# A token-parallel layout for the upper 64 features, and a deeper lag of the second matmul, in a dynamic convolution followed by a squared-ReLU feed-forward

## The chip, the core and the metric

The kernel runs on one core of a Trainium2 chip. A core has five engines that work side by side, each through its own list of instructions in order: TensorE (PE; its weight loads are shown apart as PEld), VectorE (DVE), ScalarE (ACT), GpSimd (POOL) and SyncE (SP, which only issues DMAs here). They meet through semaphores. The metric is the device time of one execution in microseconds. Before the change it is 881.08 us (median of three runs, 879.11 to 881.46).

## The reference

For 8 sequences of 4096 tokens with 192 features, each token has 8 heads of 7 weights. The weights pass through a softmax, and each output feature is the weighted sum of the feature over the token and the six before it. The result goes through a feed-forward layer with a squared ReLU.

```python
w = np.exp(weight_gen - max);  w = w / (sum(w) + 1e-09)       # [B, S, 8, 7]
out[b, s, h, g] = sum_k w[b, s, h, k] * x_pad[b, s + k, h, g]  # 8 heads of 24 features
h = np.maximum(out @ w_in, 0.0)                                # 192 -> 2048
return h * h @ w_out                                           # 2048 -> 192
```

## The kernel before

The 32768 tokens are cut into 64 blocks of 512, eight to a sequence. For each block the kernel does these stages, named as in the code.

- **Softmax** (lines 106 to 175). It runs for a whole sequence ahead of its blocks, in chunks of 8 of the 38 rows that a partition holds. `exp` is on ScalarE, `total` (a reduction) and `recip` on VectorE, and `scale` on GpSimd: it multiplies by the reciprocal and scatters the result into `v_big` (`v_small` for the first sequence, which comes in four parts of 8 rows with 14 rows each, halo included). `store` writes that to DRAM (`vd`). A chunk is done in each of a sequence's blocks 0 to 4, after the ReLUs of the block's last group.
- **st_load** fetches the block's features `xt` (on GpSimd's queue) and its weights `wr` (on SP's queue), three blocks ahead.
- **st_band** (VectorE) multiplies weights by a mask into five banded matrices `bd`, one for each stretch of about 100 tokens.
- **st_conv** (TensorE) does the convolution as 32-column matmuls against `bd`. Features 0 to 127 fill the first PSUM bank of `yp`. Features 128 to 191 are computed twice, once into partitions 0 to 63 and once into 64 to 127 of the second bank: that is 80 matmuls for a block. `st_y_evac` (ScalarE) copies both banks to SBUF as `y`.
- **st_mm1** multiplies by `w_in` in 16 chunks of 128 outputs, two chunks to a buffer `h` of two PSUM banks (a chunk pair, `fp` 0 to 7). Each chunk takes one 512-column matmul over the lower 128 features (`w_a`, line 274) and one over the upper 64 (`w_b`, line 282). The upper matmuls use half of the array's rows, and the two chunks of a pair take different halves and run at the same time.
- **st_relu** (ScalarE, line 293) and **st_sq** (VectorE, line 299) make `t1` and then `g` of a chunk pair.
- **st_mm2** (TensorE, line 310) multiplies by `w_out`: 8 matmuls of 192 columns for a chunk pair, summed in one buffer `o` of two banks. **st_o_evac** (VectorE) copies it out, and SP stores it.

The chunk pairs go in groups of (0,1,2), (3,4,5) and (6,7). There is no scheduler: the order is that of the loop in lines 368 to 404, engine by engine. TensorE does MM1 of a group, and then MM2 of the group before it. Three `h` buffers are shared in turn by the chunk pairs and `yp`, so MM1 of a pair needs the ReLU of the pair three places earlier to be done. A `g` has eight buffers, `bd` two, `o` one.

## Time and profile before

| what | value |
|---|---|
| median of 3 runs | 881.08 us (879.11 to 881.46) |
| the profiled execution | 880.54 us, of which 878.8 us is the span from first to last instruction |
| TensorE matmul busy | 796.8 us (91%), 11264 matmuls, each with a weight load of its own |
| VectorE busy | 638.2 us (73%) |
| ScalarE busy | 568.2 us (65%) |
| GpSimd busy | 147.6 us (17%) |
| mean granted TensorE clock | 0.991 |

The page gives busy shares over the whole span. A timeline (instructions in order of time, with what each engine waited for) shows the single block. A row of a timeline reads: start, duration, engine, line, operation, output and input tiles, shape, count, and in brackets the idle time just before it with what ended it. A duration of several merged matmuls includes the last one's way through the array, so the pace is taken from starts.

### The profile page before, as it was taken

To read this page: it belongs to the slowest core of one execution; us is meant where nothing else is said; L and a number is where in the kernel's file an instruction comes from. 1 tells how busy PE (TensorE), PEld (TensorE's weight loads), DVE (VectorE), ACT (ScalarE), POOL (GpSimd) and SP (SyncE) were. 2 spreads that over 40 slices of the span, in tenths; PEclk is the share of its full clock that TensorE was granted. 3 is DMA by queue.
4 is the path that set the end of the run, shared out by engine and by line. 5 is a ranking of instruction groups with operands and counts; after the bars stand their busy time and mean duration, and the time that the engine had idled before them with its cause. 6 is when DMAs were issued, how large, how long until landed. Compare 5 with 4: busy or idle time off the path is not lost.

```text
span 878.8 us, 25261 instructions
## 1 busy us (share of the span) xinstructions
PE 796.8 (91%) x11264; PEld 520.6 (59%) x11264; DVE 638.2 (73%) x979; ACT 568.2 (65%) x616; POOL 147.6 (17%) x140
## 2 busy tenths in 40 slices
PE   0678999989998999998999899998999899999997
PEld 0345666655665666665665665665666566666665
DVE  2567787687768787678777778668776878767674
ACT  0346666666676666666666666666667666666764
POOL 5332120123002220112201212012300212000000
PEclk9889999999999999999999999999999999999999
DMA  9522372232713254033622237223271225433111
GB/s 165 116 47 39 60 156 54 37 68 57 141 46 50 52 116 103 25 67 53 144 56 57 35 63 156 48 44 67 51 148 46 45 57 92 78 47 68 41 38 37
DMA packets 123789, 63.03 MB, mean 72 GB/s; under 512 B 87713, under 2 KB 121120, under 8 KB 122912
## 3 DMA queue, kind: packets, MB, share of 16 engines
q0 software_dynamic: 44480, 17.57, 18.0%
q1 hardware_dynamic: 79200, 43.84, 17.4%
q8 instruction: 88, 1.44, 0.7%
q14 instruction: 21, 0.17, 0.1%
HBM read 49.60 MB, written 29.36 MB: 90 GB/s over the span
## 4 chain that ended last, share of the span: by engine, by line
PE 45%; DVE 24%; ACT 14%; issue 13%; DMA 2%; POOL 1%; ACTq 0%; SPq 0%; DVEq 0%; POOLq 0%
PE o L310 23%; PE h L274 12%; DVE g L299 9%; ACT t L293 8%; DVE bd L223 7%; PE h L282 7%; ACT y L264 4%; DVE o_sb L320 4%; PE yp L251 3%; DVE ssum L146 3%; DVE rcp L152 2%; ACT wg L139 2%; DMA wr<-vd 1%; POOL mask L92 0%; DMA vd<-v_small 0%
## 5 line engine op out<-in xcount | busy, mean ns | idle before, releaser
L293 ACT ACTIVATE t<-h 128x1024 f16<-128x1024 f32 x512 | 489.8, 1023 | 282.3 <-PE h L282 264.9
L299 DVE TENSOR_TENSOR g<-t 128x1024 f16<-128x1024 f16 x512 | 383.1, 775 | 102.1 <-ACT t L293 102.1
L310 PE MATMUL o<-w_o,g 128*128 128x192 f16 x4096 | 380.5, 248 | 47.8 <-DVE g L299 41.6
L310 PEld LDWEIGHTS <-g 128*128 128x128 f16 x4096 | 331.8, 98 | 116.4 <-DVE g L299 81.0
L274 PE MATMUL h<-y,w_a 128*128 128x512 f16 x1024 | 259.7, 382 | 8.1 <-ACT t L293 6.9
L223 DVE TENSOR_TENSOR bd<-wr,mask 128x832 f16<-128x832 f16 (+2 forms) x320 | 171.0, 582 | 17.9 <-DMA wr<-vd 17.9
L160 POOL TENSOR_TENSOR v_big<-wg,rcp 128x448 f16<-128x448 f32 (+1 forms) x35 | 81.6, 2330 | 474.2 <-DVE rcp L152 474.2
L274 PEld LDWEIGHTS <-w_a 128*128 128x128 f16 x1024 | 97.9, 98 | 91.0 <-issue 20.0
L282 PE MATMUL h<-y,w_b 64*128 64x512 f16 x1024 | 144.5, 381 | 0.0
L146 DVE TENSOR_REDUCE ssum<-wg 128x64 f32<-128x448 f32 (+2 forms) x39 | 24.7, 633 | 110.0 <-ACT wg L139 110.0
L282 PEld LDWEIGHTS <-w_b 64*128 64x128 f16 x1024 | 34.3, 94 | 97.2 <-issue 82.2
L251 PE MATMUL yp<-bd,xt 128*32 128x104 f16 (+7 forms) x5120 | 71.1, 210 | 21.6 <-DVE bd L223 21.6
L251 PEld LDWEIGHTS <-xt 128*32 128x32 f16 (+3 forms) x5120 | 59.5, 93 | 48.8 <-issue 35.5
L213 POOL DMA_DIRECT2D xt<-in_x_dram x56 | 49.7, 887 | 170.8 <-PE yp L251 170.8
L264 ACT CAST y<-yp 128x1024 f16<-128x1024 f32 x64 | 65.1, 1018 | 19.3 <-PE yp L251 19.3
L320 DVE COPY o_sb<-o 128x768 f32<-128x768 f32 x64 | 60.8, 950 | 3.9 <-PE o L310 1.0
L139 ACT ACTIVATE wg<-wg 128x448 f32<-128x448 f32 (+2 forms) x39 | 23.6, 610 | 2.0 <-DMA wg<-in_weight_gen_dram 2.0
L152 DVE RECIPROCAL rcp<-ssum 128x64 f32<-128x64 f32 (+2 forms) x39 | 22.1, 566 | 1.7
L160 POOL TENSOR_TENSOR v_small<-wg,rcp 128x336 f16<-128x336 f32 (+1 forms) x7 | 13.0, 2025 | 15.9 <-issue 13.9
L211 POOL DMA_DIRECT2D xt<-in_x_dram x8 | 6.0, 751 | 0.0
L205 POOL DMA_DIRECT2D xt<-in_x_dram x8 | 4.8, 606 | 0.0
L92 POOL TENSOR_SCALAR_AFFINE_SELECT mask<-mask 128x104 f16<-128x104 f16 (+2 forms) x6 | 3.1, 509 | 0.4
(14 smaller groups left out, 12.4 us busy)
## 6 DMA issues: line engine op xcount, KB each, us to landing
out_dram<-o_sb SPq DMA_DIRECT2D x64, 384.0 KB, 2.8
xt<-in_x_dram POOLq DMA_DIRECT2D x56, 240.0 KB, 4.0
wg<-in_weight_gen_dram SPq DMA_DIRECT2D x6, 1064.0 KB, 8.2
wr<-vd SPq DMA_DIRECT2D x56, 80.0 KB, 3.0
vd<-v_big SPq DMA_DIRECT2D x7, 512.0 KB, 3.3
wg<-in_weight_gen_dram SPq DMA_DIRECT2D x4, 392.0 KB, 3.7
xt<-in_x_dram POOLq DMA_DIRECT2D x8, 192.0 KB, 6.2
wg<-in_weight_gen_dram SPq DMA_DIRECT2D x1, 896.0 KB, 5.8
```

What stands on the lines that cost most here:

```text
L146: nc.vector.tensor_reduce(out=self.ssum[:, i], in_=self.wg[:, i], axis=AxisX, op=AluOp.add)
L160: eng.tensor_tensor(out=bass.AP(tensor=v.tensor, offset=v.offset + i0 * H * SL, ap=[list(v.ap[0]), [H * SL + 1, n], [SL, H], [H * SL, KK]] ...
L213: eng.dma_start(out=dst, in_=rows(src, t0 + BASE, width))
L223: nc.vector.tensor_tensor(out=bd_t[j][:, H * lo : H * hi].rearrange("p (h m c) -> p h m c", h=H, c=SL), in0=wr_t[j][:, i].unsqueeze(2).bro ...
L251: nc.tensor.matmul(out=yp[p0 : p0 + m, ci, lo:hi], lhsT=x_t[j][:, i, 32 * q : 32 * q + m], rhs=bd[:, hb if later else ha, :], start=True, ...
L264: nc.scalar.copy(out=y, in_=yp_t[j])
L274: nc.tensor.matmul(out=h[:, jj, :], lhsT=w_a[:, fc * P : (fc + 1) * P], rhs=y[:, 0, :], start=True, stop=False,)
L282: nc.tensor.matmul(out=h_t[(j, fp)][:, jj, :], lhsT=w_b[r0 : r0 + LO, fc * P : (fc + 1) * P], rhs=y[r0 : r0 + LO, 1, :], start=False, stop ...
L293: nc.scalar.activation(out=t1, in_=h_t[(j, fp)], func=ActF.Relu)
L299: nc.vector.tensor_tensor(out=g, in0=t1, in1=t1, op=AluOp.mult)
L310: nc.tensor.matmul(out=o[:, c // 2, (c % 2) * Dm : (c % 2 + 1) * Dm], lhsT=g_t[(j, fp)][:, jj, c * P : (c + 1) * P], rhs=w_o[:, fc, :], st ...
L320: nc.vector.tensor_copy(out=o_sb, in_=o_t[j][:, :, 0 : 2 * Dm])
```

## The change

Five things change together.

1. The two halves of the array's rows now hold the two halves of the block's tokens for the upper 64 features, not two copies of them. `st_conv` computes features 128 to 191 once: tokens 0 to 255 go to partitions 0 to 63, and tokens 256 to 511 to partitions 64 to 127. That is 64 matmuls for a block. `y` shrinks from 1024 to 768 columns. In MM1 each chunk now takes two 256-column matmuls over the lower features and two over the upper ones, and `h`, `t1` and `g` are laid out by token half.
2. MM2 of chunk pair 5 moves behind the next block's first MM1 group: the groups of MM2 are (0,1,2), (3,4) and, late, (5,6,7). `g` has six buffers instead of eight, `bd` three instead of two.
3. In the last group of MM1 the order on TensorE is lower features, convolution of the next block, upper features; ScalarE does `y`'s copy ahead of the two ReLUs.
4. For sequences after the first, the exponential comes after the first group's ReLUs, and reduction, reciprocal and scaling come on VectorE after the second group's squares. Chunks have 8, 8, 8, 4, 4, 4 and 2 rows from sequence 2 on (a sequence's own softmax now starts two blocks earlier), and 8, 8, 8, 8, 6 for sequence 1. GpSimd keeps only the scaling of the first sequence.
5. At the start, only the first part of the weights is loaded ahead of all; `w_in` and most masks come after the first block's loads, and the second block's loads ahead of parts 2 and 3.

```diff
+    TH = TB // 2
-    p_bd = ctx.enter_context(tc.tile_pool(name="p_bd", bufs=2))
+    p_bd = ctx.enter_context(tc.tile_pool(name="p_bd", bufs=3))
-    p_g = ctx.enter_context(tc.tile_pool(name="p_g", bufs=8))
+    p_g = ctx.enter_context(tc.tile_pool(name="p_g", bufs=6))
...
+    def conv_pieces():
+        for i in range(NT):
+            lo, hi = bounds[i], bounds[i + 1]
+            for later in (True, False):
+                for q in range(4):
+                    yield later, i, q, 32 * q, 0, lo, lo, hi
+                for half in (0, 1):
+                    a, b = max(lo, TH * half), min(hi, TH * (half + 1))
+                    if a < b:
+                        for q in (4, 5):
+                            yield later, i, q, 32 * (q - 4) + LO * half, 1, a - TH * half, a, b
...
-        y = p_y.tile([P, 2, TB], f16, name="y")
+        y = p_y.tile([P, TB + TH], f16, name="y")
-        nc.scalar.copy(out=y, in_=yp_t[j])
+        nc.scalar.copy(out=y, in_=yp_t[j].rearrange("p a c -> p (a c)")[:, 0 : TB + TH])
...
+    def st_mm1_lower(j, fps):
...
+                for half in range(2):
+                    nc.tensor.matmul(
+                        out=h[:, half, jj, :],
+                        lhsT=w_a[:, fc * P : (fc + 1) * P],
+                        rhs=y[:, half * TH : (half + 1) * TH],
+                        start=(jj == 0), stop=False, skip_group_check=True,
+                    )
+    def st_mm1_upper(j, fps):
...
+                for half, r0 in enumerate((0, LO)):
+                    nc.tensor.matmul(
+                        out=h_t[(j, fp)][:, half, jj, :],
+                        lhsT=w_b[r0 : r0 + LO, fc * P : (fc + 1) * P],
+                        rhs=y[r0 : r0 + LO, TB : TB + TH],
+                        start=False, stop=(jj == 1), skip_group_check=True,
+                        tile_position=(r0, 0),
+                    )
...
-        for s in parts[:2]:
-            s.load(nc.sync)
-        load_w_in()
+        parts[0].load(nc.sync)
...
+        softmax_whole(parts[0], (nc.vector, nc.gpsimd))
+        st_load(0)
+        load_w_in()
...
+        parts[1].load(nc.sync)
+        st_load(1)
...
+        softmax_whole(parts[1], (nc.gpsimd,))
+        for s in parts[2:]:
+            s.load(nc.sync)
+        st_load(2)
...
+            st_mm1_lower(j, G0)
+            st_mm1_upper(j, G0)
+            if j:
+                st_mm2(j - 1, LATE)
+            for fp in G0:
+                st_relu(j, fp)
+            if lo < hi:
+                nxt.exp(lo, hi)
...
+            st_mm1_lower(j, G1)
+            st_mm1_upper(j, G1)
+            st_mm2(j, (0, 1, 2))
+            for fp in G1:
+                st_relu(j, fp)
+                st_sq(j, fp)
+            if lo < hi:
+                nxt.recip(lo, hi)
+                nxt.scale(lo, hi, nc.vector)
...
+            st_mm1_lower(j, G2)
+            if more:
+                st_conv(j + 1)
+                st_y_evac(j + 1)
+            st_mm1_upper(j, G2)
+            st_mm2(j, (3, 4))
```

Three places in the order of instructions matter below. The first is VectorE at the end of a block in which a chunk of softmax is done (`ssum` and `rcp` are its sums and reciprocals, `wg` the weights; L299 and L328 are the squares). Before:

```order
L299 TENSOR_TENSOR g<-t_830 128x1024
L146 TENSOR_REDUCE ssum_478<-wg_257 128x64
L152 RECIPROCAL rcp_479<-ssum_478 128x64
L299 TENSOR_TENSOR g<-t_955 128x1024
L299 TENSOR_TENSOR g<-t_957 128x1024
L223 TENSOR_TENSOR bd<-wr,mask 128x832 x2
L223 TENSOR_TENSOR bd<-wr,mask 128x768
L299 TENSOR_TENSOR g<-t_1004 128x1024
L320 COPY o_sb<-o 128x768
L299 TENSOR_TENSOR g<-t_1006 128x1024
```

With the change:

```order
L328 TENSOR_TENSOR g<-t_1130 128x1024
L144 TENSOR_REDUCE ssum_288<-wg_241 128x64
L145 RECIPROCAL rcp_289<-ssum_288 128x64
L152 TENSOR_TENSOR v_big<-wg_241,rcp_289 128x8x8x7
L328 TENSOR_TENSOR g<-t_1238 128x1024
L328 TENSOR_TENSOR g<-t_1242 128x1024
L216 TENSOR_TENSOR bd<-wr,mask 128x832 x2
L216 TENSOR_TENSOR bd<-wr,mask 128x768
L328 TENSOR_TENSOR g<-t_1301 128x1024
L328 TENSOR_TENSOR g<-t_1303 128x1024
L332 COPY o_sb<-o 128x768
```

The scaling has joined the two other steps ahead of the squares of pairs 6 and 7, and the copy of `o` stands behind a second square.

The second is ScalarE around the last group of a block (CAST is `y`'s copy, L293 and L322 are the ReLUs, L139 and L140 the exponential). Before:

```order
L293 ACTIVATE t_593<-h 128x1024
L293 ACTIVATE t_718<-h 128x1024
L293 ACTIVATE t_720<-h 128x1024
L264 CAST y<-yp 128x1024
L139 ACTIVATE wg_257<-wg_257 128x448
L293 ACTIVATE t_767<-h 128x1024
```

With the change:

```order
L322 ACTIVATE t_624<-h 128x1024
L268 CAST y<-yp 128x768
L322 ACTIVATE t_732<-h 128x1024
L322 ACTIVATE t_736<-h 128x1024
L322 ACTIVATE t_795<-h 128x1024
L322 ACTIVATE t_797<-h 128x1024
L322 ACTIVATE t_799<-h 128x1024
L140 ACTIVATE wg_241<-wg_241 128x448
```

The ReLUs of pairs 6 and 7 (`t_732`, `t_736`) now stand behind the copy, and the exponential three ReLUs later.

The third is SP's queue at the start (`wg` are loads of softmax weights, the first four of them parts 0 to 3; `vd<-v_small` are the stores of finished parts; `wr` loads belong to blocks 0, 1 and 2 in turn). Before:

```order
L124 DMA wg_104<-in_weight_gen_dram 128x784
L124 DMA wg_106<-in_weight_gen_dram 128x784
L172 DMA vd<-v_small_99 128x512
L205 DMA wr<-vd 128x64
L211 DMA wr<-vd 128x4x64
L124 DMA wg_145<-in_weight_gen_dram 128x784
L124 DMA wg_147<-in_weight_gen_dram 128x784
L213 DMA wr<-vd 128x5x64
L172 DMA vd<-v_small_100 128x512
L213 DMA wr<-vd 128x5x64
L124 DMA wg_257<-in_weight_gen_dram 128x2128
```

With the change:

```order
L125 DMA wg_104<-in_weight_gen_dram 128x784
L165 DMA vd<-v_small_99 128x512
L198 DMA wr<-vd 128x64
L204 DMA wr<-vd 128x4x64
L125 DMA wg_139<-in_weight_gen_dram 128x784
L206 DMA wr<-vd 128x5x64
L165 DMA vd<-v_small_100 128x512
L125 DMA wg_231<-in_weight_gen_dram 128x784
L125 DMA wg_233<-in_weight_gen_dram 128x784
L206 DMA wr<-vd 128x5x64
L125 DMA wg_241<-in_weight_gen_dram 128x2128
```

Block 1's weights (the first `wr` row of five stretches) now stand ahead of parts 2 and 3, and those two loads stand behind the store of part 1.

224 lines of the change are left out of this document (99 added, 125 removed).

## The prediction

> **What bounds the kernel now.** First the page: TensorE is busy for 91% of the span, so the question is what it does in the rest.
>
> ```profile
> span 878.8 us, 25261 instructions
> PE 796.8 (91%) x11264; PEld 520.6 (59%) x11264; DVE 638.2 (73%) x979; ACT 568.2 (65%) x616; POOL 147.6 (17%) x140
> PE 45%; DVE 24%; ACT 14%; issue 13%; DMA 2%; POOL 1%; ACTq 0%; SPq 0%; DVEq 0%; POOLq 0%
> ```
>
> The last row is the chain that ended last: VectorE and ScalarE hold 38% of it, so TensorE waits for them regularly. The timeline gives the beat. Each block has one run of 80 convolution matmuls:
>
> ```profile
> 65.29 1.09 PE L251 MATMUL yp<-bd,xt 128*32 128x104 f16 x80
> ...
> 405.93 1.09 PE L251 MATMUL yp<-bd,xt 128*32 128x104 f16 x80
> 419.48 1.09 PE L251 MATMUL yp<-bd,xt 128*32 128x104 f16 x80
> 432.23 1.09 PE L251 MATMUL yp<-bd,xt 128*32 128x104 f16 x80
> 444.73 1.09 PE L251 MATMUL yp<-bd,xt 128*32 128x104 f16 x80
> ...
> 858.27 1.09 PE L251 MATMUL yp<-bd,xt 128*32 128x104 f16 x80
> ```
>
> The steps are 13.55, 12.74 and 12.50 us. From 65.29 (block 2) to 858.27 (block 63) are 61 steps and 792.98 us, 13.00 on average; 65.29 lies before and 20.53 behind. A 12.50 step looks like this:
>
> ```profile
> 435.24 1.46 PE L274 MATMUL h<-y,w_a 128*128 128x512 f16 x6
> 436.63 0.82 PE L282 MATMUL h<-y,w_b 64*128 64x512 f16 x6
> 437.06 2.86 ACT L293 ACTIVATE t<-h 128x1024 f16<-128x1024 f32 x3 [2.09 <-PE h L282]
> 437.38 1.49 PE L310 MATMUL o<-w_o,g 128*128 128x192 f16 x16
> 438.71 1.03 PE L274 MATMUL h<-y,w_a 128*128 128x512 f16 x4
> 439.96 0.59 PE L274 MATMUL h<-y,w_a 128*128 128x512 f16 x2 [0.23 <-ACT t L293]
> ```
>
> Each stage starts where the last one's stream ends, but for one wait. The third pair of the middle group needs the buffer that the third ReLU frees at 437.06 + 2.86 = 439.92. Four matmuls from 438.71 take 0.86, so TensorE is ready at 439.57 and loses 0.39. Without it a block is 12.11 us. The slow step has another wait:
>
> ```profile
> 406.95 2.15 PE L310 MATMUL o<-w_o,g 128*128 128x192 f16 x24
> 407.65 1.02 ACT L264 CAST y<-yp 128x1024 f16<-128x1024 f32 x1
> 408.55 0.60 ACT L139 ACTIVATE wg<-wg 128x448 f32<-128x448 f32 x1
> 409.18 0.62 DVE L146 TENSOR_REDUCE ssum<-wg 128x64 f32<-128x448 f32 x1 [2.76 <-ACT wg L139]
> 409.83 0.55 DVE L152 RECIPROCAL rcp<-ssum 128x64 f32<-128x64 f32 x1
> 410.30 2.72 DVE L299 TENSOR_TENSOR g<-t 128x1024 f16<-128x1024 f16 x2
> 410.57 2.43 POOL L160 TENSOR_TENSOR v_big<-wg,rcp 128x448 f16<-128x448 f32 x1 [10.64 <-DVE rcp L152]
> 413.07 0.83 PE L310 MATMUL o<-w_o,g 128*128 128x192 f16 x8 [1.16 <-DVE g L299]
> ```
>
> The squares of pairs 6 and 7 stand behind a reduction that waits for an exponential that waits for `y`'s copy. The two squares then take 2.72 us, with GpSimd's scaling beside them. MM2 waits 1.16 for the second. This is the 1.05 us between 13.55 and 12.50.
>
> **The change, part by part: matmuls.** The pace of a stream is its starts. Six matmuls of 512 columns span 1.46 us and four 1.03, so one takes (1.46 − 1.03)/2 = 0.215, and a single one's own length is 0.38. For 192 columns it is (1.49 − 0.25)/15 = 0.083, 0.25 being the single one's length in this row of the page (busy, mean ns of one; its weight loads below it):
>
> ```profile
> L310 PE MATMUL o<-w_o,g 128*128 128x192 f16 x4096 | 380.5, 248 | 47.8 <-DVE g L299 41.6
> L310 PEld LDWEIGHTS <-g 128*128 128x128 f16 x4096 | 331.8, 98 | 116.4 <-DVE g L299 81.0
> ```
>
> On the line through both, 256 columns take 0.109. The lower features cost 32 × 0.109 instead of 16 × 0.215, or +0.05 a block. The upper ones: three pairs of 512 start 0.22 apart ((0.82 − 0.38)/2); 256 columns less are 0.106 less, so 16 pairs at 0.114 stand against 8 at 0.22, +0.06. The convolution loses 16 of 80 matmuls, but these ran beside others in other column tiles; only in the stretch that spans both halves do two pieces of 48 columns run side by side where 96 ran, twice: −0.04. Modes of the array change as often as before (seven times a block). So 12.11 becomes **12.18**: the layout by itself saves TensorE nothing.
>
> That the 16 extra `w_b` loads are hidden rests on two rows:
>
> ```profile
> 427.87 0.11 PEld L282 LDWEIGHTS <-w_b 64*128 64x128 f16 x4 [0.42 <-issue]
> 428.11 0.10 PEld L282 LDWEIGHTS <-w_b 64*128 64x128 f16 x2
> ```
>
> Four loads are done in 0.11 us, and the next two start when the second pair of matmuls does and end 0.10 later, just inside the 0.114 that a pair will last. If the cover failed, see the rival below.
>
> **The buffer waits.** An `h` buffer is free 439.96 − 436.63 = 3.33 us after the upper matmuls of its group start. Into the middle group TensorE now arrives after 0.77 (six upper pairs and the change of mode; 437.38 − 436.63 = 0.75 before) + 24 × 0.083 + 8 × 0.109 = 3.63, with no wait: pair 5's MM2 fills the gap, and the 0.39 goes. Into the last group it arrives after 0.77 + 1.99 + 0.44 = 3.20 and waits **0.13**. Next late is the first group of the next block. ScalarE's copy starts some 1.10 after the convolution does. It costs between 1.02 (as before) and 0.82: 256 columns less at 0.00077 each, from the exponential's 0.60 for 448 columns and 0.858 for 784:
>
> ```profile
> L139 ACT ACTIVATE wg<-wg 128x784 f32<-128x784 f32 x4 | 3.3, 858 | 2.0 <-DMA wg<-in_weight_gen_dram 2.0
> ```
>
> I take 0.82, since duration follows size there. The ReLUs of pairs 6 and 7, ready earlier, stand behind it and follow at 0.92 ((2.86 − 1.02)/2); the second is over at 1.10 + 0.72 + 0.92 + 1.02 = 3.76 and its buffer free at 3.80. TensorE wants that buffer after the convolution (0.98: 406.95 − 405.93 = 1.02 with its change of mode, less 0.04), four upper pairs and a change (0.54), 16 matmuls of MM2 (1.32) and eight of 0.109 (0.88), at 3.72: a wait of **0.08**. A block comes to 12.18 + 0.21, say **12.40**; with a copy of 1.02 it would be 12.60.
>
> **The softmax.** GpSimd's scaling and its collision with the squares go. VectorE gets it instead. Its price is known from one instruction at the start, beside GpSimd's for the same shape:
>
> ```profile
> L160 POOL TENSOR_TENSOR v_big<-wg,rcp x35: 1864/2423/2466, 49.6 to 737.4; 128x448 f16<-128x448 f32 x28, 128x336 f16<-128x336 f32 x7
> L160 DVE TENSOR_TENSOR v_small<-wg,rcp x1: 2153/2153/2153, 6.8 to 6.8; 128x448 f16<-128x448 f32 x1
> ```
>
> The bounds are 0.62 (the reduction over as many elements) and 2.47 (GpSimd's longest); I take the row of the same engine and shape, 2.15. The Trainium skill, "VectorE: DVE Perf Modes", section "The TRN2 errata — SBUF-src ops pay a fixed extra latency per instruction", has fp32 tensor_tensor at (N + 151)/0.96 ns, an estimated 0.62 us here; the measured 2.15 for this scattered output speaks against it, and the page's figure would only take rival B away. VectorE's load in a plain block:
>
> ```profile
> 444.73:457.23 12.50, 12.27 (x179) 8.05 (x177) 8.70 (x14) 8.55 (x10) 0.85 (x1) 1.00 0.34 60
> ```
>
> (columns: PE, PEld, DVE, ACT, POOL busy.) 8.70 for its 14 instructions, plus 0.62 + 0.55 + 2.15 = 12.02 of 12.40 in a block with eight rows; there are 4 + 6 × 3 = 22 of these, and the others have room. Nobody waits: the 3.32 us start after the square of pair 5, delay the square of pair 7 to about 1.8 us into the next block, and MM2 of pair 7 comes at 3.5, since pair 5 and 6 go first; the bands and two squares behind it are done by 4.7, the copy of `o` by 5.6, and MM2 of pair 0, which needs them, starts at 6.3. The exponential (0.60) lies between the third ReLU, over 3.3 us after the first group's upper matmuls start, and the fourth, ready 0.43 (437.06 − 436.63) after the second group's do, at 0.77 + 1.99 + 8 or more matmuls of 0.109 and so past 4.5. So 61 steps of 12.40 are 756.4 instead of 793.0: **−36.6**.
>
> **The start.** Two rows of groups (a reduction of a whole part; a part's load, with its us to landing), then the timeline:
>
> ```profile
> L146 DVE TENSOR_REDUCE ssum<-wg 128x112 f32<-128x784 f32 x4 | 3.8, 951 | 5.1 <-ACT wg L139 5.1
> wg<-in_weight_gen_dram SPq DMA_DIRECT2D x4, 392.0 KB, 3.7
> ...
> 9.41 1.69 POOL L160 TENSOR_TENSOR v_small<-wg,rcp 128x336 f16<-128x336 f32 x1
> 24.23 1.01 ACT L264 CAST y<-yp 128x1024 f16<-128x1024 f32 x1 [19.32 <-PE yp L251]
> 28.03 3.71 POOL L160 TENSOR_TENSOR v_small<-wg,rcp 128x448 f16<-128x448 f32 x2 [13.93 <-issue]
> 37.10 1.56 DVE L223 TENSOR_TENSOR bd<-wr,mask 128x832 f16<-128x832 f16 x3 [5.96 <-DMA wr<-vd]
> 39.32 4.02 PE L310 MATMUL o<-w_o,g 128*128 128x192 f16 x24 [6.48 <-DVE g L299]
> 53.88 3.98 DVE L223 TENSOR_TENSOR bd<-wr,mask 128x832 f16<-128x832 f16 x3
> 59.38 4.00 PE L310 MATMUL o<-w_o,g 128*128 128x192 f16 x24 [4.32 <-DVE o_sb L320]
> ```
>
> GpSimd's scaling of six rows of part 0 no longer waits for the masks, but now collides with VectorE's of eight: in turn from 6.8 they end at 6.8 + 2.15 + 1.69 = 10.6 against 11.1, and I give the first load, now alone in its queue, another 0.5. So the first copy comes at 23.2. Block 1's bands no longer wait until 37.10 for `wr`. But part 2's load now stands behind the store of part 1, whose scaling ends near 30.7 (31.74 before). The load lands some 3.7 later, and its exponential (0.86) is in front of block 0's ReLUs on ScalarE: these start near 35.5. Reduction (0.95) and a reciprocal that I put at about as much bring the bands to 37.3, now beside GpSimd's scaling of part 2, where three of them take 3.98 as at 53.88. MM2 of block 0 starts near 41.9 instead of 39.3. In block 1 the same collision comes again, and the copy of `o` is one square later: 60.4 instead of 59.38. Block 2's convolution then falls at **65.9** (65.29 before: the 5.9 from 59.38 on, less 0.4 for the later place in the group), 62 to 70 if loads land 4 us sooner or later. The end keeps its 20.5 less the lost wait: 20.4, since pair 5's MM2 runs while the last squares are made.
>
> Sum: 65.9 + 756.4 + 20.4 = 842.7 for the span; 1.7 lies around it (880.54 − 878.8), and the median was 0.5 above the profiled run: **844.9 us**.
>
> **Rivals.** A is the forecast, with 12.2 to 12.6 a block: 833 to 857 by the block alone, 829 to 861 with the start.
>
> B: **VectorE becomes the bound** in the eight-row blocks. It decides above 12.40 − 9.87 = 2.53 for the scaling, close to GpSimd's 2.47. At 3.5 us, 22 × 0.97 = 21 us: 866. For it: three such blocks follow each other, so delay adds up. Against: the row of 2.15, taken while GpSimd ran too.
>
> C: **the change does not do what it says**, and the squares of pairs 6 and 7 are late as before, because more work stands ahead of them. With all of the 1.05 in the 22 blocks and half in the 18 of four rows, 31 × 1.05 = 33: 878. Against: the 1.7 us between pair 7's square and its MM2.
>
> D, the other side: **weight loads one after another.** If the 32 upper loads of a block took turns at the pace of MM2's (331.8/4096 = 0.081), the upper features would last 2.59 instead of 1.82 us, +0.77 × 63 = 49: 893, slower. All of the gain (36.6 over 61 blocks of 16 pairs, 0.037 a pair) is gone from 0.151 a pair on. For it: 0.10 a load against 0.114 is tight. Against: the four loads in 0.11. The Trainium skill, "TensorE: Matmul & The Clock Gate", section "Back-to-back issue gap", states this mechanism as a rule, a spacing set by load and matmul together, about 81 ns each at 128 columns; by that rule the estimate is the same 893, and the trace agrees for MM2 but not for row tiles.
>
> E: no buffer waits remain: 12.18 a block, 831, or 827 with a start 4 us quicker.
>
> **How the numbers follow.** A 0.70, B 0.09, C 0.06, D 0.08, E 0.07. The range 829 to 864 takes in A and parts of B and E, 0.79. Differences under 0.3% (2.6 us) can't be told from none. Faster: A, B, E and most of C, 0.90; within 0.3%: 0.02, from C; slower: D, 0.08.
>
> **What would show it.** Right: convolutions 12.3 to 12.5 us apart whether or not softmax falls in the block; no MM2 waits for squares after block 2; short waits of MM1 for ReLUs; pairs of `w_b` matmuls 0.11 apart; VectorE's scaling near 2.15. Wrong: a scaling over 2.5 with MM2 waiting behind it (B), pairs 0.16 apart (D), or block 2's convolution far from 66.

## The result and the profile after

| | before | after |
|---|---|---|
| median | 880.81 us (4 runs, 879.11 to 881.46) | 826.62 us (4 runs, 826.17 to 826.70) |
| ratio, with its 95% interval | 1 | 0.9387 (0.937 to 0.9403) |
| span of the profiled execution | 878.8 us | 825.0 us |
| TensorE matmul busy | 796.8 us (91%) | 782.1 us (95%) |

The change is faster by 54 us. The forecast was 844.9 us (829 to 864): the direction was right, but the gain was 18 us larger than foretold, and the time lies 2.4 us below the range.

The page of the changed kernel, the span, the busy time of the engines and their shares of the chain that ended last:

```profile
span 825.0 us, 27303 instructions
PE 782.1 (95%) x12288; PEld 661.6 (80%) x12288; DVE 679.1 (82%) x1050; ACT 555.9 (67%) x628; POOL 78.9 (10%) x105
PE 92%; DVE 3%; DMA 2%; POOL 1%; issue 0%; ACT 0%; SPq 0%; POOLq 0%; DVEq 0%; ACTq 0%
```

TensorE held 45% of the chain before and holds 92% now. VectorE and ScalarE, with 38% before, have almost left it, although VectorE is busier than it was (679.1 us against 638.2). The timeline gives the beat again, by the first matmul of each convolution:

```profile
65.36 0.97 PE L255 MATMUL yp<-bd,xt 128*32 128x104 f16 x64
...
428.76 0.97 PE L255 MATMUL yp<-bd,xt 128*32 128x104 f16 x64
440.87 0.97 PE L255 MATMUL yp<-bd,xt 128*32 128x104 f16 x64
...
804.27 0.97 PE L255 MATMUL yp<-bd,xt 128*32 128x104 f16 x64
```

All 61 steps from block 2 on take 12.11 us, whether a block has eight rows of softmax, fewer or none. Together they are 738.9 us (804.27 − 65.36); 65.36 lies before and 20.73 behind. Busy time in the two blocks from 428.76 (columns: length, then PE, PEld, DVE, ACT and POOL, clock and DMA) shows what sets it:

```profile
428.76:440.87 12.11, 12.11 (x193) 10.27 (x192) 11.59 (x18) 8.81 (x10) 0.86 (x1) 1.00 0.36 63
440.87:452.99 12.12, 12.12 (x195) 10.29 (x194) 11.60 (x18) 8.63 (x10) 0.86 (x1) 1.00 0.35 61
```

A matmul is under way all the time. VectorE, at 11.60, has half a microsecond left. The block that begins at 428.76, in the timeline of TensorE and ScalarE (chosen rows):

```profile
429.66 0.61 PE L293 MATMUL h<-y,w_b 64*128 64x256 f16 x8
429.77 0.80 ACT L268 CAST y<-yp 128x768 f16<-128x768 f32 x1 [1.44 <-PE yp L255]
430.21 1.49 PE L311 MATMUL o<-w_o,g 128*128 128x192 f16 x16
430.47 1.95 ACT L322 ACTIVATE t<-h 128x1024 f16<-128x1024 f32 x2
431.54 1.53 PE L280 MATMUL h<-y,w_a 128*128 128x256 f16 x12
433.00 0.83 PE L293 MATMUL h<-y,w_b 64*128 64x256 f16 x12
433.76 2.15 PE L311 MATMUL o<-w_o,g 128*128 128x192 f16 x24
435.75 1.47 PE L280 MATMUL h<-y,w_a 128*128 128x256 f16 x12
437.59 2.86 ACT L322 ACTIVATE t<-h 128x1024 f16<-128x1024 f32 x3 [0.84 <-PE h L293]
439.90 1.04 PE L280 MATMUL h<-y,w_a 128*128 128x256 f16 x8
```

One wait is left, and it is so short that no bracket shows it: the twelve lower matmuls of the first group take 1.53 us (431.54), those of the middle group 1.47 (435.75). That is the third pair, which needs the buffer of pair 7: its ReLU is over at 430.47 + 1.95 = 432.42, and eight matmuls of 0.109 after 431.54 TensorE is ready at 432.41. It starts 0.05 later, and that wait is the 0.055 a block of the text below.

### The profile page after: what moved, and what is told of

Same layout as the page of the kernel before. It is cut to its first block, busy times and chain, and to the rows that moved or that the text cites. A ratio compares the mean times of both kernels' runs of the same rounds, so it can differ in the third digit from the quotient of the medians.

```text
span 825.0 us, 27303 instructions
## 1 busy us (share of the span) xinstructions
PE 782.1 (95%) x12288; PEld 661.6 (80%) x12288; DVE 679.1 (82%) x1050; ACT 555.9 (67%) x628; POOL 78.9 (10%) x105
## 3 DMA queue, kind: packets, MB, share of 16 engines
q1 hardware_dynamic: 79200, 43.84, 18.6%
## 4 chain that ended last, share of the span: by engine, by line
PE 92%; DVE 3%; DMA 2%; POOL 1%; issue 0%; ACT 0%; SPq 0%; POOLq 0%; DVEq 0%; ACTq 0%
PE o L311 43%; PE h L280 27%; PE h L293 16%; PE yp L255 7%; DVE bd L216 1%; DMA wr<-vd 1%; DMA wg<-in_weight_gen_dram 1%; DVE g L328 1%; POOL v_small L152 1%; DVE ssum L144 1%; DVE rcp L145 0%; DMA vd<-v_small 0%; ACT wg L140 0%; DVE o_sb L332 0%; DVE v_big L152 0%
## 5 line engine op out<-in xcount | busy, mean ns | idle before, releaser
L322 ACT ACTIVATE t<-h 128x1024 f16<-128x1024 f32 x512 | 490.3, 1025 | 133.1 <-PE h L293 130.0
L328 DVE TENSOR_TENSOR g<-t 128x1024 f16<-128x1024 f16 x512 | 353.1, 697 | 111.5 <-ACT t L322 108.2
L280 PE MATMUL h<-y,w_a 128*128 128x256 f16 x2048 | 261.4, 274 | 11.0 <-ACT t L322 10.1
L280 PEld LDWEIGHTS <-w_a 128*128 128x128 f16 x2048 | 198.4, 98 | 35.4 <-issue 11.6
L293 PE MATMUL h<-y,w_b 64*128 64x256 f16 x2048 | 145.2, 271 | 0.0
L268 ACT CAST y<-yp 128x768 f16<-128x768 f32 x64 | 51.1, 799 | 115.0 <-PE yp L255 115.0
L293 PEld LDWEIGHTS <-w_b 64*128 64x128 f16 x2048 | 84.2, 94 | 41.5 <-issue 27.6
L255 PE MATMUL yp<-bd,xt 128*32 128x104 f16 (+14 forms) x4096 | 63.8, 208 | 21.3 <-DVE bd L216 21.3
L152 DVE TENSOR_TENSOR v_big<-wg,rcp 128x448 f16<-128x448 f32 (+3 forms) x47 | 74.8, 1591 | 1.6
L144 DVE TENSOR_REDUCE ssum<-wg 128x64 f32<-128x448 f32 (+4 forms) x51 | 26.2, 514 | 14.0 <-ACT wg L140 14.0
L140 ACT ACTIVATE wg<-wg 128x448 f32<-128x448 f32 (+4 forms) x51 | 25.9, 508 | 14.0 <-DMA wg<-in_weight_gen_dram 14.0
```

The lines of the kernel that those rows point to most:

```text
L144: nc.vector.tensor_reduce(out=ssum, in_=self.wg[:, lo:hi], axis=AxisX, op=AluOp.add)
L152: eng.tensor_tensor(out=bass.AP(tensor=v.tensor, offset=v.offset + lo * H * SL + lo % SL, ap=[list(v.ap[0]), [H * SL + 1, n], [SL, H], [H ...
L255: nc.tensor.matmul(out=yp[p0 : p0 + m, ci, col : col + b - a], lhsT=x_t[j][:, i, 32 * q : 32 * q + m], rhs=bd[:, hb if later else ha, a - ...
L268: nc.scalar.copy(out=y, in_=yp_t[j].rearrange("p a c -> p (a c)")[:, 0 : TB + TH])
L280: nc.tensor.matmul(out=h[:, half, jj, :], lhsT=w_a[:, fc * P : (fc + 1) * P], rhs=y[:, half * TH : (half + 1) * TH], start=(jj == 0), stop ...
L293: nc.tensor.matmul(out=h_t[(j, fp)][:, half, jj, :], lhsT=w_b[r0 : r0 + LO, fc * P : (fc + 1) * P], rhs=y[r0 : r0 + LO, TB : TB + TH], sta ...
```

## The experiments

Each run changes the kernel before or the changed kernel in a few places. The step between two convolutions in the steady part tells more than the whole time, and is the same to 0.01 us in nearly all plain blocks of a run. A softmax step is one with eight rows.

| kernel | step, us | median, us | ratio to before (95%) |
|---|---|---|---|
| before | 12.50, softmax blocks 13.55 | 881 | |
| before, layout alone | 12.43, softmax 13.36 | 871.66 | 0.9896 (0.9881 to 0.9911) |
| before, later pair 5 alone | 12.55, softmax 13.56 | 882.49 | 1.0015 (1.0006 to 1.0024) |
| before, moved softmax alone | 12.50 | 850.67 | 0.9662 (0.9646 to 0.9678) |
| before, these two | 12.55 | 852.43 | 0.9678 (0.9663 to 0.9692) |
| before, these two and the early copy of y | 12.40 | 845.18 | 0.9596 (0.9577 to 0.9614) |
| **changed kernel** (the last plus the layout, the new start, other chunk sizes and buffer counts) | 12.11 | 826.62 | 0.9387 (0.937 to 0.9403) |
| changed, early copy undone | 12.40 | 844.36 | 0.9583 (0.9567 to 0.9599) |
| changed, later pair 5 undone | 12.43 | 845.96 | 0.9602 (0.9588 to 0.9616) |
| changed, copy of 1024 columns | 12.33 | 839.51 | 0.9529 (0.9515 to 0.9543) |
| changed, scaling on GpSimd | 12.11 | 825.90 | 0.9379 (0.9363 to 0.9395) |
| changed, 80 conv matmuls | 12.20 | 832.84 | 0.9457 (0.944 to 0.9473) |
| changed, other start | 12.11 | 805.54 | 0.9145 (0.9127 to 0.9163) |
| other start, copy of y between the ReLUs | 12.06 | 802.69 | 0.9109 (0.9095 to 0.9124) |

### One part at a time, added to the kernel before

The expectations weigh a Theory 1: the change gained by removing two waits, the 0.39 us before the middle group and the 1.16 us for the squares, and the layout by itself is worth little. The new start (part 5 of the change) and the sizes of the softmax chunks were not tried by themselves. Block 2's convolution comes at 65.29 us before and at 65.36 with the change, so no gain of the new start shows there.

**The layout alone.** Convolution pieces, `y`, `h`, `t1` and `g` by token halves; stages, softmax and start in the old order, so the change's two functions for MM1 are called one behind the other. Part of the edit:

```diff
-        y = p_y.tile([P, 2, TB], f16, name="y")
+        y = p_y.tile([P, TB + TH], f16, name="y")
...
+    def st_mm1(j, fps):
+        st_mm1_lower(j, fps)
+        st_mm1_upper(j, fps)
```

> The kernel before with the token halves alone (conv pieces, 768-column copy of y, MM1 and its buffers by halves, MM2 reading them); order of the stages, softmax and start as before. Theory 1 (the layout is worth little; what the change gained were waits): the conv is 0.11 us shorter, the lower and upper features stay as long within 0.05, the waits of 0.39 us for the third ReLU and of 1.16 us for the squares stay, so blocks 12.4 us instead of 12.50 and the whole 865 to 875. Rival (the layout is the main gain, because a block is TensorE's work and the layout cuts it): 850 or less. Rival by the prediction's own figure (+0.07 us a block): 880 to 886.

Measured: 871.66 us, plain steps of 12.43 and softmax steps of 13.36 instead of 12.50 and 13.55. Theory 1 holds. The convolution is 0.11 shorter (its 64 matmuls start within 0.76 us, 80 before within 0.875); both old waits are still there (that for pair 7's square is 1.03 us instead of 1.16), so the layout brings 9 us and no more.

**The later pair 5 alone.**

```diff
-                if before:
-                    st_mm2(*before)
+                if gi == 0 and j:
+                    st_mm2(j - 1, (5, 6, 7))
+                elif gi:
+                    st_mm2(j, ((0, 1, 2), (3, 4))[gi - 1])
```

> The kernel before with one thing changed: MM2 of pair 5 goes to the next block (MM2 of pairs 5, 6, 7 behind the first group, 0 to 2 behind the second, 3 and 4 behind the third); old layout, softmax steps as before, on GpSimd. Theory 1 (the gain is the sum of the two waits removed): the 0.39 us wait before the middle group goes in all blocks, and the wait for pair 7's square shrinks by the 0.66 us that eight more matmuls of MM2 last, from 1.16 to about 0.5; plain blocks 12.11 us, softmax blocks 12.6 to 12.9, the whole 838 to 853, 845 likeliest. Rival (the lag only moves the stall): plain blocks stay at 12.5 and the whole over 870.

Measured: 882.49 us, nothing gained. Theory 1 falls. The wait before the middle group did go, but a new one of nearly the same length stands before the first group. In the timeline of this kernel, in a softmax block:

```profile
406.29 1.94 ACT L293 ACTIVATE t<-h 128x1024 f16<-128x1024 f32 x2 [0.91 <-PE h L282]
406.40 1.09 PE L251 MATMUL yp<-bd,xt 128*32 128x104 f16 x80
407.42 1.49 PE L310 MATMUL o<-w_o,g 128*128 128x192 f16 x16
408.12 1.02 ACT L264 CAST y<-yp 128x1024 f16<-128x1024 f32 x1
409.19 1.45 PE L274 MATMUL h<-y,w_a 128*128 128x512 f16 x6 [0.28 <-ACT y L264]
...
413.55 0.83 PE L310 MATMUL o<-w_o,g 128*128 128x192 f16 x8 [0.72 <-DVE g L299]
```

The 8 matmuls of MM2 that left the block had covered the copy of `y`. Now 16 follow the convolution instead of 24; they are through 1.33 us after 407.42, at 408.75, and MM1 starts at 409.19: a wait of 0.44, because the copy stands behind the two ReLUs of the last group (406.29 + 1.94). The wait for the square of pair 7 did shrink, from 1.16 to 0.72, by just these 0.44 us.

**The moved softmax alone.** The exponential behind the first group's ReLUs; reduction, reciprocal and scaling, on VectorE, behind the middle group's squares.

```diff
+                step = nxt and jb < len(nxt.chunks())
+                if gi == 0 and step:
+                    nxt.exp(nxt.chunks()[jb])
...
-                if gi == NG - 1 and nxt and jb < len(nxt.chunks()):
...
-                    nxt.scale(i0, nc.gpsimd)
...
+                if gi == 1 and step:
+                    i0 = nxt.chunks()[jb]
+                    nxt.total(i0)
+                    nxt.recip(i0)
+                    nxt.scale(i0, nc.vector)
```

> The kernel before with one thing changed: the exponential goes behind the first group's ReLUs, and reduction, reciprocal and scaling behind the middle group's squares, the scaling on VectorE; old layout, MM2 order as before. Theory 1: no wait for squares any more, but the 0.39 us stays, so every block takes 12.50 us with softmax or without, and the whole 847 to 856. Rival (without the later pair 5, VectorE's 3.3 us in the new place make the squares of pairs 6 and 7 late for MM2, which then comes first in the next block): softmax blocks 13 us or more, 860 to 880.

Measured: 850.67 us and 12.50 in all 61 steps. Theory 1 holds: the softmax has no price any more, −30 us, more than half of the whole gain. The other wait is untouched, in this kernel's timeline as before:

```profile
382.68 1.03 PE L274 MATMUL h<-y,w_a 128*128 128x512 f16 x4
383.94 0.59 PE L274 MATMUL h<-y,w_a 128*128 128x512 f16 x2 [0.23 <-ACT t L293]
```

**These two together**, the last two edits in one kernel.

```diff
+                    st_mm2(j - 1, (5, 6, 7))
...
+                    st_mm2(j, ((0, 1, 2), (3, 4))[gi - 1])
...
+                    nxt.scale(i0, nc.vector)
```

> The kernel before with both, the later pair 5 and the moved softmax on VectorE, in the old layout and with the old start. Theory 1 (the change gained by removing two waits, and its layout by itself next to nothing): every block 12.11 us, the whole 825 to 832, level with the changed kernel's 826.6. Rival (the layout has a share of the gain, because its conv is 0.11 us shorter and nothing gives that back): 833 to 838. Rival (the two waits are one and the same, so that the parts do not add): about as the better of the two parts alone, over 838.

Measured: 852.43 us, 12.55 in all steps. Theory 1 had said 825 to 832 and falls a second time, and with it the reading that the change removed two waits and that its layout adds nothing. The block ends with the wait for `y` just shown (0.44 instead of 0.39). What Theory 1 had left out is part 3 of the change, the order in the last group: convolution and copy of `y` first, upper matmuls and ReLUs after. This is **Theory 2**: a stall moves to whatever is late next, and it takes the later pair 5, the early copy and the short copy together to have next to none of it left. The four runs that follow were made for it.

### Theory 2: the stall wanders until the copy of y is early and short

**All of the order, in the old layout:** the two edits above and, new, this one (`st_mm1_lower` and `st_mm1_upper` are the two halves of `st_mm1`).

```diff
-                st_mm1(j, fps)
+                st_mm1_lower(j, fps)
                 if gi == NG - 1 and j + 1 < NBLK:
                     st_conv(j + 1)
...
+                    st_y_evac(j + 1)
+                st_mm1_upper(j, fps)
...
-                if gi == NG - 1 and j + 1 < NBLK:
-                    st_y_evac(j + 1)
```

> The kernel before with all of the change's order in the old layout: later pair 5, softmax moved to VectorE, and (new against the last run) the convolution and the copy of y ahead of the third group's upper matmuls and ReLUs, as in the changed kernel. Theory 2 (the stall only wanders until the copy of y comes early and is short): the 0.44 us wait for y goes, but the copy of 1024 columns still takes 1.02 us, so that the ReLU of pair 7 ends some 3.99 us behind the convolution's start while TensorE wants its buffer at 3.74; with 0.05 from the ReLU's end to the matmul a wait of 0.28, blocks of 12.39 us, the whole 838 to 848. Rival 1 (order is all, the layout is worth next to nothing): blocks of 12.11, the whole 825 to 831. Rival 2 (the swap does nothing): 850 to 854 as before it.

**The early copy undone** in the changed kernel.

```diff
+            st_mm1_upper(j, G2)
             if more:
                 st_conv(j + 1)
-                st_y_evac(j + 1)
-            st_mm1_upper(j, G2)
             st_mm2(j, (3, 4))
             for fp in G2:
                 st_relu(j, fp)
+            if more:
+                st_y_evac(j + 1)
+            for fp in G2:
                 st_sq(j, fp)
```

> The changed kernel with one thing undone: the convolution goes back behind the third group's upper matmuls, and the copy of y behind the ReLUs of pairs 6 and 7. Theory 2: the copy of y ends 2.57 us behind the convolution's start, TensorE is there at 2.24, so a wait of about 0.33 us before the first group in every block and no other; blocks of 12.38, the whole 838 to 847. Rival (the place of the copy does not matter, since the 16 matmuls of MM2 behind the convolution cover it): 826 to 829.

**The later pair 5 undone** in the changed kernel.

```diff
-    LATE = (5, 6, 7)
+    LATE = (6, 7)
...
-            st_mm2(j, (3, 4))
+            st_mm2(j, (3, 4, 5))
```

> The changed kernel with one thing undone: MM2 of pair 5 goes back into its own block (pairs 6 and 7 behind the first group, 3 to 5 behind the third). Theory 2 (with the copy early, the place of pair 5's MM2 decides which group waits): the wait of about 0.36 us for the third ReLU before the middle group is back, the 0.055 before the first group goes; blocks of 12.42, the whole 842 to 852. Rival 1 (the lag is worth nothing, as it was alone in the old order): 826 to 830. Rival 2 (the lag is what hides the softmax on VectorE): softmax blocks over 13 us and the whole over 855.

**A longer copy** in the changed kernel.

```diff
-        y = p_y.tile([P, TB + TH], f16, name="y")
+        y = p_y.tile([P, 2, TB], f16, name="y")
...
-        nc.scalar.copy(out=y, in_=yp_t[j].rearrange("p a c -> p (a c)")[:, 0 : TB + TH])
+        yp = yp_t[j]
+        nc.scalar.copy(
+            out=y,
+            in_=bass.AP(
+                tensor=yp.tensor, offset=yp.offset, ap=[list(yp.ap[0]), [TH, 2], [1, TB]]
+            ),
+        )
...
-                        rhs=y[r0 : r0 + LO, TB : TB + TH],
+                        rhs=y[r0 : r0 + LO, 1, TH:TB],
```

> The changed kernel with the copy of y made 1024 columns long instead of 768 (columns 256 to 511 are copied twice; nothing else changes, and the result is the same). Theory 2: the ReLU of pair 7 ends 0.22 us later and the wait of the first group's third pair grows from 0.055 to 0.27, blocks of 12.33, the whole 837 to 842. Rival (a longer copy is hidden, as the other work of ScalarE is, whose busy share is two thirds): 826 to 828.

Measured, in this order: 845.18, 844.36, 845.96 and 839.51 us; steps of 12.40, 12.40, 12.43 and 12.33, against 12.39, 12.38, 12.42 and 12.33 expected. Each wait is where Theory 2 puts it. Four pieces of timelines, of these four kernels in turn, with the copy or the lower matmuls in which it hides:

```profile
425.16 1.01 ACT L264 CAST y<-yp 128x1024 f16<-128x1024 f32 x1 [1.55 <-PE yp L251]
426.07 1.95 ACT L296 ACTIVATE t<-h 128x1024 f16<-128x1024 f32 x2
426.91 1.75 PE L274 MATMUL h<-y,w_a 128*128 128x512 f16 x6
```

```profile
426.42 1.49 PE L311 MATMUL o<-w_o,g 128*128 128x192 f16 x16
427.23 0.81 ACT L268 CAST y<-yp 128x768 f16<-128x768 f32 x1
428.09 1.47 PE L280 MATMUL h<-y,w_a 128*128 128x256 f16 x12 [0.18 <-ACT y L268]
```

```profile
431.35 1.04 PE L280 MATMUL h<-y,w_a 128*128 128x256 f16 x8
432.60 0.60 PE L280 MATMUL h<-y,w_a 128*128 128x256 f16 x4 [0.21 <-ACT t L322]
```

```profile
422.56 1.01 ACT L269 CAST y<-yp 128x1024 f16<-128x1024 f32 x1 [1.45 <-PE yp L255]
423.47 1.95 ACT L328 ACTIVATE t<-h 128x1024 f16<-128x1024 f32 x2
424.32 1.74 PE L286 MATMUL h<-y,w_a 128*128 128x256 f16 x12
```

The first: in the old layout six lower matmuls take 1.75 us instead of 1.46, 0.29 of waiting for pair 7's ReLU, which a copy of 1024 columns delays. The second: MM1 starts 1.67 after MM2 does, where 1.33 is the work of 16 matmuls (430.21 to 431.54 in the changed kernel): 0.34 of waiting for the copy. The third: 0.38 between eight lower matmuls that are through at 431.35 + 0.87 and the next. The fourth differs from the changed kernel only in the length of one ScalarE instruction, 1.01 instead of 0.80 us, and in where `y`'s columns lie, and pays 0.22 us in each block, 13 us in all: that instruction lies on the path, on an engine that is idle a third of the time. So the layout, worth 9 us alone, is worth 0.29 us a block, or 17.7 us over 61 steps, as the last part to come: 0.055 for TensorE's own work and 0.235 for the shorter copy. The medians are 18.6 us apart (845.18 and 826.62); these two kernels also differ in the start, the chunk sizes and the buffer counts, and the 0.9 us that is left is within the noise.

### The other disputed terms

**Scaling on GpSimd, in its new place.**

```diff
-                nxt.scale(lo, hi, nc.vector)
+                nxt.scale(lo, hi, nc.gpsimd)
```

> The changed kernel with one thing undone: the batch softmax is scaled by GpSimd again, in its new place behind the middle group's squares. Theory 2 (the place counts, not the engine): the scaling on GpSimd runs from some 1.5 to 4.5 us behind the convolution's start and slows the squares of pairs 6 and 7, which are then over by 5.5, while MM2 of pair 7 asks for its square at 6.2; blocks stay at 12.11 and the whole at 825 to 829. Rival (the collision of the scaling with the squares was what cost the old kernel its softmax blocks, 2.72 us for two squares): at least half a microsecond in the 27 blocks with six to eight rows, the whole over 838.

Measured: 825.90 us, steps of 12.11. Theory 2 holds: in the changed kernel the place counts, not the engine. (In the old order the new place was tried only with the scaling on VectorE. The blocks with six to eight rows are 23 in this kernel, not 27; that leaves the rival near 838 and refuted.) The collision is still there, but nobody waits for it:

```profile
416.93 2.22 POOL L152 TENSOR_TENSOR v_big<-wg,rcp 128x448 f16<-128x448 f32 x1 [22.21 <-DVE rcp L145]
418.08 1.69 DVE L328 TENSOR_TENSOR g<-t 128x1024 f16<-128x1024 f16 x2 [1.29 <-ACT t L322]
```

**Sixteen more convolution matmuls** in the changed kernel, into columns that nobody reads.

```diff
                         for q in (4, 5):
                             yield later, i, q, 32 * (q - 4) + LO * half, 1, a - TH * half, a, b
+                    else:
+                        for q in (4, 5):
+                            yield later, i, q, 32 * (q - 4) + LO * half, 1, TH, lo, hi
```

> The changed kernel with 16 more convolution matmuls a block (80 as before, the added ones write columns that nobody reads, in column tiles that the others leave free at that moment; nothing else changes, and the result is the same). Theory 2 (the convolution is paced by its number of matmuls, 11 ns each, as 80 starts in 0.875 us before and 64 in 0.761 now suggest, and not by the columns that the array must pass): blocks 0.11 us longer, the whole 832 to 835. Rival (columns set the pace, and the added matmuls run beside others as the prediction took it, at 0.04 us a block): 826 to 829.5.

Measured: 832.84 us, steps of 12.20. The rival falls: matmuls in column tiles that others leave free are not free. But Theory 2's price was too high as well. The step is 0.09 longer. The convolution's starts now span 0.840 us, 0.079 more, which is 5 ns for each added matmul, not 11. Of the 0.114 between 80 and 64 matmuls, 0.079 comes with the sixteen matmuls, and 0.035 stays with what else differs (pieces of 48 columns where one of 96 ran). What sets the 5 ns is open.

**Another start.** Its core (the order of TensorE's stages in the loop is kept):

```diff
+    p_wp = ctx.enter_context(tc.tile_pool(name="p_wp", bufs=4))
...
         parts[0].load(nc.sync)
+        parts[1].load(nc.sync)
...
+        st_load(0, "x")
         load_w_in()
...
+        soft(parts[1], two)
+        parts[1].store(nc.sync)
+        parts[3].load(nc.sync)
...
         st_y_evac(0)
         load_w_out()
+        parts[2].exp(0, parts[2].rh)
+        soft(parts[2], two)
...
-            if j < 2:
-                softmax_whole(parts[2 + j], (nc.gpsimd,))
-            if j + 3 < NBLK:
-                st_load(j + 3)
+            if j + 2 < NBLK:
+                st_load(j + 2, "xw")
```

> The changed kernel with another start, the loop over the blocks in its order: four buffers for the parts' weights, so that parts 1 to 3 are loaded long before their exponentials; weights of MM1 and x of block 0 loaded ahead of the first scaling; softmax of parts 1 and 2 in VectorE's idle time before and behind the first bands, and of part 3 in block 0; loads of blocks two ahead instead of three; the second batch's softmax in blocks 1 to 5 and stored one block later. Theory 2 (of the 65.36 us before block 2's convolution some 18 are TensorE waiting: 10.06 for the ReLUs behind part 2's late exponential, 4.09 for the copy of o behind bands slowed by GpSimd, the rest for wr behind the weight loads): convolution of block 2 at 46 to 54 us, blocks as before 12.11, the whole 808 to 816. Rival 1 (TensorE's slow first microseconds set the start, so that earlier data only moves the wait): 820 to 827. Rival 2 (the softmax on VectorE in blocks 0 and 1 and the later store of a batch stall the blocks): over 827.

Measured: 805.54 us, 21 less than the changed kernel. Block 2's convolution comes at 44.63 us, earlier than the expected 46 to 54, so the whole lies 2.5 us below Theory 2's range: both rivals fall, but Theory 2 expected too little. It changes several things at once, so the 21 us can't be divided among them. From block 1 on every step is 12.11. The first lower matmuls of block 0, the first of three short waits behind them, the longest wait before block 1, and block 1's convolution, in this kernel's timeline:

```profile
20.08 2.72 PE L280 MATMUL h<-y,w_a 128*128 128x256 f16 x12 [0.89 <-ACT y L268]
24.46 0.60 PE L280 MATMUL h<-y,w_a 128*128 128x256 f16 x4 [0.36 <-ACT t L322]
29.57 2.14 PE L311 MATMUL o<-w_o,g 128*128 128x192 f16 x24 [1.92 <-DMA w_o<-in_moe_w_out_dram]
32.51 0.97 PE L255 MATMUL yp<-bd,xt 128*32 128x104 f16 x64
```

**The copy of y between the two ReLUs**, on top of that start.

```diff
+            st_mm1_upper(j, G2)
             if more:
                 st_conv(j + 1)
-                st_y_evac(j + 1)
-            st_mm1_upper(j, G2)
             st_mm2(j, (3, 4))
-            for fp in G2:
-                st_relu(j, fp)
-                st_sq(j, fp)
+            st_relu(j, 6)
+            if more:
+                st_y_evac(j + 1)
+            st_relu(j, 7)
+            st_sq(j, 6)
+            st_sq(j, 7)
```

> The kernel with the new start, and in the third group the convolution back behind the upper matmuls, but ScalarE's order now ReLU of pair 6, copy of y, ReLU of pair 7. Theory 2 (what counts is when ScalarE is done with the copy and with pair 7's ReLU, not where the convolution stands on TensorE): the ReLU of pair 6 runs while the convolution does, the copy ends 1.86 us behind the convolution's start (TensorE asks at 2.24) and pair 7's ReLU at 2.8 (asked at 3.1), so neither the 0.055 of the changed kernel nor the 0.34 of the run with the convolution put back; blocks of 12.05 to 12.06 us and the whole 801 to 803.5. Rival 1 (the convolution's place on TensorE is what counts): a wait of 0.3 us again and 820 or more. Rival 2 (the 0.055 is no wait for the ReLU but part of TensorE's own work): 805 to 806.

Measured: 802.69 us, steps of 12.06. Theory 2 holds to the hundredth. TensorE's order in the block is that of the run with the early copy undone, which waited 0.34; in the block only ScalarE's order differs (the start is the other one), and no wait is left:

```profile
418.17 1.02 ACT L322 ACTIVATE t<-h 128x1024 f16<-128x1024 f32 x1 [0.87 <-PE h L293]
419.18 1.49 PE L311 MATMUL o<-w_o,g 128*128 128x192 f16 x16
419.29 0.80 ACT L268 CAST y<-yp 128x768 f16<-128x768 f32 x1
419.99 1.03 ACT L322 ACTIVATE t<-h 128x1024 f16<-128x1024 f32 x1
420.51 1.47 PE L280 MATMUL h<-y,w_a 128*128 128x256 f16 x12
```

This is the best version of the study, 79 us below the kernel before. Its 12.06 is also the price of the new layout without any wait.

## Why the prediction was wrong, and where it was right

The sum was 65.9 + 61 × 12.40 + 20.4; measured were 65.36 + 61 × 12.11 + 20.73. Start and end are off by 0.5 and 0.3. All of the miss lies in the block, 0.29 × 61 = 17.7 us; that put the time below the range. It has four terms.

- **The wait of 0.13 into the last group: the step that failed.** The prediction gave pair 7 the buffer of pair 5. The row of the middle group's ReLUs (437.59, 2.86 long) ends at 440.45; the lower matmuls of pairs 6 and 7 start at 439.90, eight in one row, and the fifth, pair 7's first, 4 × 0.109 later, at 440.34, before that ReLU is over. It can't have been waiting for it. Had it needed that buffer, it would have waited some 0.1 us, as foretold. There are three buffers, and pairs 6 and 7 start before this one is free, so it is left for the convolution, which comes next and starts only at 440.87. The wait was 0, and 0.13 was overcharged.
- **The convolution, −0.04.** It was −0.114. The prediction counted columns of the array and let extra matmuls run beside others at no cost; the run with 80 matmuls shows that 16 of them cost 0.079. This and the wait of 0.13 are seven tenths of the miss.
- **Lower and upper features, +0.11 together.** They came to +0.06: 12.11 − 0.114 + 0.06 = 12.06, as the last run shows without any wait. The lower price was right (0.109 for 256 columns, +0.05). The upper one was too high: eight upper matmuls take 0.61 us (429.66) and twelve 0.83 (433.00), so a pair takes 0.11 and not 0.114, and 16 pairs cost about what 8 of 0.22 did, not 0.06 more. So "the layout by itself saves TensorE nothing" was wrong by 0.12 a block.
- **The wait of 0.08 into the next block's first group** was right in its mechanism and place and is 0.055. The longer copy gave the price that the prediction had named for it, 0.2 a block, and the reordered copy removed the wait.

0.13 + 0.074 + 0.05 + 0.025 is 0.28 of the 0.29; the rest is 12.39 put as 12.40. Rival E, no buffer waits, came nearest; it was given 0.07, because the buffer of pair 7 was reasoned from the order of the loop. That its 827 is so close is partly luck: it takes a block of 12.18 and a start 4 us quicker, while the kernel keeps a wait of 0.055, has 0.12 less work on TensorE, and starts no quicker.

What was right, by the prediction's steps:

- **The softmax**: VectorE's scaling takes 2.18 us (2.15 foretold), no MM2 waits for a square after block 2, and the step is the same in softmax blocks. Rival B is refuted by 11.60 of 12.11. That the scaling should leave GpSimd, which the prediction took as part of the gain, was unnecessary.
- **The 0.39 goes**: true of the whole change, but the reason given, that pair 5's MM2 fills the gap, is only half of it. Alone it moved the wait to the copy of `y`. The prediction had the early copy in its sum (as the time at which the copy starts, 1.10 after the convolution, 1.01 measured) without pricing what its absence would cost: 0.34 a block.
- **Weight loads**: rival D is refuted. Twelve loads of `w_b` take 0.55 us in block 1:

```profile
50.95 0.55 PEld L293 LDWEIGHTS <-w_b 64*128 64x128 f16 x12 [0.21 <-issue]
50.95 0.83 PE L293 MATMUL h<-y,w_b 64*128 64x256 f16 x12
```

  With the serial pace of 0.081 they would take 0.97. The spacing rule of the Trainium skill, "TensorE: Matmul & The Clock Gate", section "Back-to-back issue gap", which the prediction weighed, does not hold for the two row tiles here.
- **The start** came out at 65.36 for 65.9, but by errors that cancel: block 0's ReLUs came 1.7 us later than foretold (37.21 for 35.5), its MM2 1.9 later (43.76 for 41.9), and block 1's MM2 0.4 earlier (60.04 for 60.4). The two waits are those foretold:

```profile
36.45 0.86 ACT L140 ACTIVATE wg<-wg 128x784 f32<-128x784 f32 x1 [11.03 <-DMA wg<-in_weight_gen_dram]
37.21 2.83 ACT L322 ACTIVATE t<-h 128x1024 f16<-128x1024 f32 x3
38.27 2.84 PE L280 MATMUL h<-y,w_a 128*128 128x256 f16 x12 [10.06 <-ACT t L322]
...
60.04 4.00 PE L311 MATMUL o<-w_o,g 128*128 128x192 f16 x24 [4.09 <-DVE o_sb L332]
```

  The prediction saw that part 2's load would stand behind the store of part 1 and took it as a price. The run with the other start, which takes that load and several others forward, gains 21 us.

## What to carry to other kernels

Undo each part of a change and also do each alone: here one part, the later pair 5, was worth nothing alone and 19 us as the last to come (845.96 to 826.62), because a removed stall only hands over to the next one until all are gone. When several instructions share buffers in turn, read from the trace which one really had to wait (a matmul that starts before a ReLU ends did not need that ReLU's buffer), since the loop's order does not tell it. And once one engine is busy all the time, look where it is not yet: here the start still held 21 us.

## What the runs showed of the hardware

- **Idle time at the start was followed by slow matmuls.** The granted clock (the column behind POOL's busy time) fell in and after the waits of 10 and 4 us in the changed kernel, and the work behind the second ran at about half speed: 24 matmuls of MM2 took 4.00 us at 60.04, 2.15 elsewhere. Behind the first wait, twelve lower matmuls took 2.84 us at 38.27, against 1.47 in the steady part. No run varied an idle time by itself, so that the wait brings the clock down is read from this order of events.

```profile
28.00:38.20 10.20, 0.20 (x4) 0.10 (x1) 1.65 (x2) 1.75 (x3) 3.64 (x3) 0.64 0.64 164
...
56.00:60.00 4.00, 0.00 (x0) 0.10 (x1) 4.00 (x6) 1.96 (x3) 3.37 (x4) 0.77 0.21 37
60.00:65.36 5.36, 5.32 (x33) 4.46 (x32) 5.29 (x9) 0.55 (x1) 0.00 (x0) 0.54 1.22 181
```

  In the run with the other start the column reads 1.00 in every stretch from 14 us on, and yet its first twelve lower matmuls take 2.72 us (20.08), nearly twice 1.47; from 24.46 on they run at the steady pace. At the very start the column can't be taken as the pace; the matmuls' own times tell it.
- **Matmuls spread over four column tiles start 11 to 12 ns apart on average** (64 in 0.76 us, 80 in 0.84 to 0.875). The Trainium skill, "TensorE: Matmul & The Clock Gate", section "Wait — 56ns, not 53.3ns?", gives about 25 ns as the least spacing of starts however small a matmul is; here the measurement decides, and over the four tiles together it is under half of that. From one matmul to the next in the same tile it is more than that: at 440.87 four start within 0.01 us, one in each tile, and the next four about 0.05 later.
- **A square that starts under GpSimd's scaling ends with it.** With the scaling on GpSimd in its new place, the scaling ends at 416.93 + 2.22 = 419.15 and the two squares, 1.28 long where nothing collides, at 419.77, which is the end of the scaling and most of one square. The Trainium skill, "SBUF — State Buffer", section "Who interferes with whom", says that such a VectorE instruction is blocked until GpSimd's is over; these rows, and the two squares of 2.72 us in the kernel before, which end 0.02 after the scaling (410.30 + 2.72 against 410.57 + 2.43), agree. The prediction spoke of a collision only, and the expectation for the scaling on GpSimd of squares that are slowed.
